# Attention and a two-product layer on one core: weights converted four tiles at a time, and the switch to three-product arithmetic made earlier

## The chip, the core and the metric

The program runs on one core of a Trainium2 chip. The core has a matrix engine (PE), a vector engine (DVE), a scalar engine (ACT), GpSimd (POOL) and a queue engine (SP) that issues the DMAs. Each engine works through its own list of instructions in order; semaphores hold an instruction until another engine or a DMA has done its part. The metric is the device time of one execution in microseconds, lower is better.

## The reference

```python
def _attn_ref(q, k, v):                # 8 batches, 8 heads, 576 positions, 64 wide
    scores = 1/sqrt(64) * q @ k.T      # heads 0-3: a causal window of 32
    scores = where(masks, scores, -1e9)  # heads 4-7: 128 wide, every 4th position
    attn = softmax(scores)
    return attn @ v

x = attention output as (4608, 512)
h = x @ w_in                           # (512, 2048)
g = where(h > 0, h, exp(min(h, 0)) - 1)
out = g @ w_out                        # (2048, 512)
```

The weights come to the chip as 64-bit floating-point numbers and are made into 32-bit numbers by integer operations on their two halves.

## The kernel before, in words

**Chunks and tiles.** The 4608 rows of x are worked through as nine chunks (c = 0 to 8) of 512. The 2048 hidden columns are sixteen tiles (f = 0 to 15) of 128. For each chunk and tile `gemm1` makes the 128x512 hidden block h in one PSUM bank (h0 or h1), `elu` makes g of it, and `gemm2` adds g's product with the rows f of w_out into four PSUM banks (o_ps), two tiles later (LAG = 2): the order on PE is gemm1 of tile f, then gemm2 of tile f - 2. After a chunk's sixteenth gemm2, `store` copies the four banks out on ACT (L420) into buffers `o`, and SP sends each to memory (L421). The attention of batch c + 1 is worked in between, as pieces behind chosen tiles of chunk c: the tuple `when` (L508) names the tiles behind which the scores of head pairs 0 and 1, their outputs, the scores of pairs 2 and 3, and their outputs stand. A scores piece has two halves on PE; between them stands a one-element copy on ACT, `nothing` (L326), which the second half waits for.

**Two kinds of product.** A product of 32-bit numbers is either one plain matrix product, or three of numbers split into a high part (rounded to fp32r) and the rest (low): high by high, high by low, low by high. `split_w` makes the two parts of a weight (a cast on ACT, L136, a subtraction on DVE, L137), `split_x` those of x (L363, L364), and the end of `elu` those of g (`gh` on ACT, L405, `gl` on DVE, L406). In chunk 0 the first products use plain ones below tile F1 = 9 and the second below F2 = 14; all others use three.

**Converting.** `load_w(k)` loads a "pair" k: two 128x512 blocks of weights, in the order in which they are needed (mostly the w_in of tile k + 1 and the w_out of tile k - 1). `magnitude(k)` takes the upper words' absolute value on ACT (L103, 128x1024), `convert(k)` has four DVE operations of 128x1024 (L111, L113, L114, L116). The raw words lie in eight buffers r0 to r7, four of which hold inputs of the first attention before; pair 8 is loaded over pair 0's once that is converted. In chunk 0 the loop converts up to AHEAD = 4 tiles ahead. What chunk 0 leaves unsplit is split in chunk 1.

**What sets the order.** The framework lays every engine's list out beforehand by a timeline of its own; `inorder` keeps an instruction in program order, and `tc.issue_after` puts one behind another. PE's products are all in program order. Tiles of a pool (`fp` for e, gh, gl, h, o) come from buffers in turn, and the first writer of a buffer waits for the last reader before.

## Time and profile before

| what | value |
|---|---|
| median of 3 runs | 904.67 us (904.6 to 905.83) |
| the profiled execution, its own time | 905.6 us |
| its span, first to last instruction | 903.7 us |
| PE busy | 883.6 us (98%) |
| DVE busy | 581.0 us (64%) |
| ACT busy | 376.7 us (42%) |
| mean granted PE clock | 0.996 |

The profiled execution took 0.93 us more than the median, and 1.9 us of it lie around the span. A PE busy share counts pipelined products by ends that are modelled, so PE's pace is read from the distance between starts.

### The profile page before, as it was taken

How to read it: one execution, taken by the hardware profiler on the slowest of the kernel's cores; microseconds unless marked ns; L12 is line 12 of the kernel's file. 1: busy time of each engine (PE TensorE's matmuls, PEld its weight loads, DVE VectorE, ACT ScalarE, POOL GpSimd, SP SyncE). 2: the span in 40 equal slices, each digit the busy share in tenths (PEclk: the TensorE clock that was granted, in tenths of full speed). 3: DMA queues.
4: the chain of work that ended last, by engine and by line, in shares of the span. 5: the costliest groups of instructions: out<-in, count | busy, mean ns of one | idle time of the engine just before them, and what ended most of it. 6: DMA issues, size and time to landing. Idle time of an engine off the chain costs nothing.

```text
span 903.7 us, 15468 instructions
## 1 busy us (share of the span) xinstructions
PE 883.6 (98%) x6540; PEld 695.3 (77%) x6540; DVE 581.0 (64%) x999; ACT 376.7 (42%) x750; POOL 6.0 (1%) x12
## 2 busy tenths in 40 slices
PE   6899999999999999999999999999999999999998
PEld 4544657788878887888788878888788888888886
DVE  5899999966485847694687559574859433343332
ACT  3755767434533343434443343434434432233222
POOL 2000000000000000000000000000000000000000
PEclk8999999999999999999999999999999999999999
DMA  9964103020122013111202111210210010001001
GB/s 341 406 228 145 45 19 100 19 90 1 43 94 89 2 36 102 36 55 36 102 7 84 36 48 54 90 34 2 102 37 1 1 47 1 1 0 47 1 1 46
DMA packets 23796, 59.35 MB, mean 66 GB/s; under 512 B 2640, under 2 KB 2736, under 8 KB 23728
## 3 DMA queue, kind: packets, MB, share of 16 engines
q1 hardware_dynamic: 23728, 58.37, 18.9%
q8 instruction: 51, 0.84, 0.4%
q14 instruction: 17, 0.14, 0.0%
HBM read 48.92 MB, written 9.44 MB: 65 GB/s over the span
## 4 chain that ended last, share of the span: by engine, by line
PE 82%; DVE 8%; DMA 5%; issue 2%; ACT 2%; SPq 0%; ACTq 0%; DVEq 0%
PE h L83 41%; PE o_ps L83 38%; PE a_ps L83 3%; DMA r<-w_out 2%; DVE a L116 1%; DVE a L114 1%; DMA out<-o 1%; DVE a L111 1%; DVE pt L304 1%; DMA r<-w_in 1%; DVE gh L397 1%; DVE r L137 1%; ACT o L420 1%; DVE a L113 1%; DMA kt<-k 1%
## 5 line engine op out<-in xcount | busy, mean ns | idle before, releaser
L83 PE MATMUL o_ps<-a,gh 128*128 128x512 f32 x816 | 267.8, 418 | 0.0
L83 PE MATMUL h<-xh,r 128*128 128x512 f32 x792 | 266.2, 394 | 0.5 <-DVE gh L397 0.5
L83 PEld LDWEIGHTS o_ps<-a,gh 128*128 128x128 f32 x816 | 152.8, 188 | 50.4 <-issue 22.0
L401 DVE TENSOR_SCALAR e<-e 128x512 f32<-128x512 f32 x128 | 54.6, 426 | 191.8 <-ACT e L392 189.9
L83 PEld LDWEIGHTS h<-xh,r 128*128 128x128 f32 x792 | 148.6, 188 | 35.6 <-DVE gh L397 2.1
L83 PE MATMUL h<-xl,r 128*128 128x512 f32 x412 | 160.6, 390 | 0.0
L405 ACT CAST gh<-e 128x512 fp32r<-128x512 f32 x130 | 80.9, 622 | 177.0 <-DVE e L402 176.7
L83 PE MATMUL o_ps<-a,gl 128*128 128x512 f32 x352 | 136.9, 389 | 0.0
L406 DVE TENSOR_TENSOR gl<-e,gh 128x512 fp32r<-128x512 f32 x130 | 89.6, 689 | 71.9 <-ACT gh L405 41.5
L392 ACT ACTIVATE e<-h 128x512 f32<-128x512 f32 x144 | 89.4, 621 | 103.6 <-PE h L83 100.9
L390 ACT COPY h<-h 128x512 f32<-128x512 f32 x96 | 56.2, 585 | 117.7 <-PE h L83 117.6
L304 DVE STREAM_TRANSPOSE pt<-sm 32x384 f32<-32x384 f32 x168 | 95.4, 568 | 2.2
L83 PE MATMUL o_ps<-r,gh 128*128 128x512 f32 x304 | 96.2, 389 | 0.0
L402 DVE SCALAR_TENSOR_TENSOR e<-h,e 128x512 f32<-128x512 f32 x128 | 88.2, 689 | 3.5
L83 PEld LDWEIGHTS h<-xl,r 128*128 128x128 f32 x412 | 77.3, 188 | 17.0 <-issue 1.2
L83 PE MATMUL h<-xh,a 128*128 128x512 f32 x256 | 85.5, 395 | 0.0
L83 PEld LDWEIGHTS o_ps<-a,gl 128*128 128x128 f32 x352 | 66.1, 188 | 13.8
L83 PEld LDWEIGHTS o_ps<-r,gh 128*128 128x128 f32 x304 | 57.1, 188 | 11.8
L83 PE MATMUL o_ps<-r,gl 128*128 128x512 f32 x168 | 65.5, 390 | 0.3 <-DVE gl L406 0.3
L83 PEld LDWEIGHTS h<-xh,a 128*128 128x128 f32 x256 | 48.0, 188 | 11.0
L83 PE MATMUL h<-xl,a 128*128 128x512 f32 x128 | 50.0, 391 | 0.0
L289 ACT ACTIVATE sm<-sm 96x768 f32<-96x768 f32 x24 | 20.4, 849 | 45.0 <-DVE sm L288 45.0
(100 smaller groups left out, 751.4 us busy)
## 6 DMA issues: line engine op xcount, KB each, us to landing
vt<-v SPq DMA_DIRECT2D x30, 384.0 KB, 3.6
kt<-k SPq DMA_DIRECT2D x30, 304.0 KB, 4.6
qt<-q SPq DMA_DIRECT2D x30, 288.0 KB, 3.8
r<-w_in SPq DMA_DIRECT2D x16, 512.0 KB, 8.0
r<-w_out SPq DMA_DIRECT2D x16, 512.0 KB, 8.2
out<-o SPq DMA_DIRECT2D x32, 256.0 KB, 2.8
out<-xl SPq DMA_DIRECT2D x4, 256.0 KB, 2.1
r<-v SPq DMA_DIRECT2D x2, 384.0 KB, 8.3
```

The lines of the kernel that those rows point to most:

```text
L83: return inorder(nc.tensor.matmul(*args, **kw))
L111: keep(nc.vector.tensor_scalar(out=a, in0=a, scalar1=TINY, scalar2=None, op0=ALU.max))
L113: keep(nc.vector.tensor_scalar(out=au, in0=au, scalar1=0x07FFFFFF, scalar2=3, op0=ALU.bitwise_and, op1=ALU.logical_shift_left))
L114: keep(nc.vector.scalar_tensor_tensor(out=au, in0=hi, scalar=0xC0000000, in1=au, op0=ALU.bitwise_and, op1=ALU.bitwise_or))
L289: nc.scalar.activation(out=sm, in_=sm, func=AF.Exp, scale=0.125)
L304: last_transpose[b] = nc.vector.transpose(out=tr[ks, :, cs], in_=sm[cs, :, rs]).ins
L390: nc.scalar.copy(out=h, in_=h_ps)
L392: nc.scalar.activation(out=e, in_=h_ps, func=AF.Exp)
L401: nc.vector.tensor_scalar(out=e, in0=e, scalar1=1.0, scalar2=-1.0, op0=ALU.min, op1=ALU.add)
L402: nc.vector.scalar_tensor_tensor(out=e, in0=h_ps, scalar=0.0, in1=e, op0=ALU.max, op1=ALU.add)
L405: nc.scalar.copy(out=gh, in_=e)
L406: nc.vector.tensor_tensor(out=gl, in0=e, in1=gh.bitcast(F32), op=ALU.subtract)
```

## The change

Three groups of edits.

*Conversion by two pairs.* The raw words now lie in four buffers of two pairs each (NR = 4), and so do the converted weights (a0 to a7). `convert(j)` works on pairs 2j and 2j + 1 in one set of four operations of 128x2048. Pairs 0 and 1 are still converted in pieces before tile 0's products, pairs 2 and 3 in two pieces of 128x1024 behind the hidden block of tile 0. `magnitude` stays at one operation for each pair. AHEAD goes from 4 to 3 and the loop advances by two tiles. Both pairs of a buffer are loaded once the buffer's whole set of earlier readers is done.

*Three products earlier.* F1 goes from 9 to 7 and F2 from 14 to 11. Weights of two more first products and three more second products are split in chunk 0, and tiles 11 to 13 of chunk 0 get their `gl`. Chunk 1's splits wait in addition for a hidden block of late in chunk 0.

*Later chunks.* For chunks 2 to 6 the attention pieces stand behind tiles 2, 7, 8 and 13 (before 1, 6, 7 and 12). The buffers for `e` are four and serve the output copies as well, where there were three for each.

```diff
@@ -34,8 +34,8 @@
 NC = DM // P
-AHEAD = 4
-NR = NF // 2
-NE = 4
+AHEAD = 3
+NR = NF // 4
+NE = 2
 LAG = 2
-F1 = 9
-F2 = 14
+F1 = 7
+F2 = 11
 NEG = -1.0e9
@@ -52,3 +52,3 @@
     xp = ctx.enter_context(tc.tile_pool(name="xp", bufs=1))
-    fp = ctx.enter_context(tc.tile_pool(name="fp", bufs=3))
+    fp = ctx.enter_context(tc.tile_pool(name="fp", bufs=4))
     ps_first = ExitStack()
@@ -67,3 +67,4 @@
-    early = [wst.tile([P, 4 * DM], F32, name=f"r{NR - NE + i}") for i in range(NE)]
+    early2 = [wst.tile([P, 2, 4 * DM], F32, name=f"r{NR - NE + i}") for i in range(NE)]
+    early = [early2[i // 2][:, i % 2, :] for i in range(2 * NE)]
     for z in pt:
@@ -71,3 +72,3 @@
-    raw, full2, full = [None] * NF, [None] * NF, [None] * 2 * NF
+    raw2, raw, full4, full2, full = [None] * (NF // 2), [None] * NF, [None] * (NF // 2), [None] * NF, [None] * 2 * NF
@@ -86,3 +87,5 @@
-        raw[k] = wst.tile([P, 2, DM], I64, name=f"r{k % NR}")
+        if k % 2 == 0:
+            raw2[k // 2] = wst.tile([P, 4, DM], I64, name=f"r{k // 2 % NR}")
+        raw[k] = raw2[k // 2][:, k % 2 * 2:k % 2 * 2 + 2, :]
         if behind is not None:
@@ -93,5 +96,5 @@
-    def halves(k):
+    def words(j):
-        u = raw[k].rearrange("p t c -> p (t c)").bitcast(U32).rearrange("p (c two) -> p c two", two=2)
+        u = raw2[j].rearrange("p t c -> p (t c)").bitcast(U32).rearrange("p (c two) -> p c two", two=2)
         return u[:, :, 0], u[:, :, 1]
@@ -99,11 +102,14 @@
     def magnitude(k):
-        pair = full2[k] = wst.tile([P, 2, DM], F32, name=f"a{k}")
+        j, part = k // 2, slice(k % 2 * 2 * DM, (k % 2 + 1) * 2 * DM)
+        if k % 2 == 0:
+            full4[j] = wst.tile([P, 4, DM], F32, name=f"a{j}")
+        full2[k] = full4[j][:, k % 2 * 2:k % 2 * 2 + 2, :]
         for t in range(2):
-            full[need[2 * k + t]] = pair[:, t, :]
-        return nc.scalar.activation(out=pair.rearrange("p t c -> p (t c)"), in_=halves(k)[1].bitcast(F32), func=AF.Abs)
+            full[need[2 * k + t]] = full2[k][:, t, :]
+        return nc.scalar.activation(out=full4[j].rearrange("p t c -> p (t c)")[:, part], in_=words(j)[1][:, part].bitcast(F32), func=AF.Abs)
-    def convert(k, keep=lambda ins: ins, part=slice(0, 2 * DM)):
+    def convert(j, keep=lambda ins: ins, part=slice(0, 4 * DM)):
-        lo, hi = [u[:, part] for u in halves(k)]
-        a = full2[k].rearrange("p t c -> p (t c)")[:, part]
+        lo, hi = [u[:, part] for u in words(j)]
+        a = full4[j].rearrange("p t c -> p (t c)")[:, part]
         au = a.bitcast(U32)
@@ -118,3 +124,3 @@
-    spaces = [[f"r{i}", 4] for i in range(NR)] + [["a-1", 2]]
+    spaces = [["a-1", 4]] + [[f"r{i}", 8] for i in range(NR)]
     taken = {}
@@ -139,4 +145,4 @@
             wh[need[2 * k + t]], wl[need[2 * k + t]] = h[:, t - t0, :], l[:, t - t0, :]
-        if all(wh[need[2 * k + t]] is not None for t in range(2)):
-            spaces.append([f"a{k}", 2])
+        if all(wh[need[k // 2 * 4 + t]] is not None for t in range(4)):
+            spaces.append([f"a{k // 2}", 4])
@@ -386,3 +392,3 @@
     def elu(h_ps, c, f):
-        e = fp.tile([P, TC], F32, name="e", bufs=3)
+        e = fp.tile([P, TC], F32, name="e")
         if 0 < c < B - 1:
@@ -418,3 +424,3 @@
         for t in range(TC // P):
-            o = fp.tile([P, DM], F32, name="o", bufs=3) if c < NCH - 1 else xp.tile([P, DM], F32, name=f"xl{t}")
+            o = fp.tile([P, DM], F32, name="e") if c < NCH - 1 else xp.tile([P, DM], F32, name=f"xl{t}")
             nc.scalar.copy(out=o, in_=o_ps[t])
@@ -473,3 +479,3 @@
         elif what[0] in "BCD":
-            last_conversion = convert(i, inorder, {"B": slice(0, DM), "C": slice(DM, 2 * DM), "D": slice(0, 2 * DM)}[what[0]])
+            last_conversion = convert(i // 2, inorder, {"B": slice(0, DM), "C": slice(DM, 2 * DM), "D": slice(2 * DM, 4 * DM)}[what[0]])
         elif what[0] == "G":
@@ -484,3 +490,3 @@
     load_v(NPAIR)
-    for j in range(NR - NE, NR + 2):
+    for j in range(2 * (NR - NE), 2 * NR + 2):
         load_w(j)
@@ -507,12 +513,15 @@
-        when = () if c == 0 or c >= B - 1 else (0, 6, 7, 13) if c == 1 else (1, 6, 7, 12)
+        when = () if c == 0 or c >= B - 1 else (0, 6, 7, 13) if c == 1 else (2, 7, 8, 13)
         for f in range(NF):
             while c == 0 and ready < min(NF, f + AHEAD):
-                with tc.issue_after(below[-1] if below else last_copy.ins):
-                    magnitude(ready)
-                with tc.issue_after(last_conversion.ins):
-                    last_conversion = convert(ready)
-                if ready + NR < NF:
-                    load_w(ready + NR)
-                ready += 1
+                for j in (ready, ready + 1):
+                    with tc.issue_after(below[-1] if below else last_copy.ins):
+                        magnitude(j)
+                if f > 0:
+                    with tc.issue_after(last_conversion.ins):
+                        last_conversion = convert(ready // 2)
+                for j in (ready, ready + 1):
+                    if j + 2 * NR < NF:
+                        load_w(j + 2 * NR)
+                ready += 2
             if c == 0 and f == F1 - 3:
@@ -523,3 +532,3 @@
-                with tc.issue_after(last_transpose[1] if split < 2 else last_x):
+                with tc.issue_after(last_transpose[1] if split < 2 else last_x), tc.issue_after(hidden[-3]):
                     if left:
@@ -528,2 +537,7 @@
             pend.append((c, f, elu(gemm1(c, f), c, f)))
+            if (c, f) == (0, 0):
+                for part in slice(0, 2 * DM), slice(2 * DM, 4 * DM):
+                    with tc.issue_after(last_conversion.ins), tc.issue_after(hidden[-1]):
+                        last_conversion = convert(1, part=part)
             if c == 0 and F1 <= f + 2 <= NF:
```

On **ACT**, around the end of chunk 2 and the start of chunk 3 (`h` copies and `e` exponentials belong to hidden blocks, `o` or `e<-o_ps` are the output copies of the chunk just ended). Before:

```order
L392 ACTIVATE e<-h 128x512 [waits Activation_49]
L405 CAST gh<-e 128x512 [waits DVE_49]
L390 COPY h<-h_3229 128x512 [waits PE_49]
L392 ACTIVATE e<-h 128x512 [waits Activation_49]
L420 COPY o<-o_ps 128x512 [waits DMAHW0_49,PE_49]
L420 COPY o<-o_ps 128x512 [waits DMAHW1_49,PE_49]
L420 COPY o<-o_ps 128x512 [waits DMAHW2_49,PE_49]
L405 CAST gh<-e 128x512 [waits DVE_49]
L420 COPY o<-o_ps 128x512 [waits DMAHW7_49,PE_49,Activation_49]
L326 COPY nothing<-h_3278 96x1 [waits PE_49]
L289 ACTIVATE sm<-sm 96x768 [waits DVE_49]
```

With the change:

```order
L396 COPY h<-h_3222 128x512 [waits PE_49]
L398 ACTIVATE e<-h 128x512 [waits Activation_49]
L426 COPY e<-o_ps 128x512 [waits PE_49] x2
L426 COPY e<-o_ps 128x512 [waits DVE_49,PE_49]
L411 CAST gh<-e 128x512 [waits DVE_49]
L426 COPY e<-o_ps 128x512 [waits DMAHW7_49,PE_49,Activation_49]
L396 COPY h<-h_3269 128x512 [waits PE_49]
L398 ACTIVATE e<-h 128x512 [waits DVE_49,Activation_49]
L411 CAST gh<-e 128x512 [waits DVE_49]
L332 COPY nothing<-h_3310 96x1 [waits PE_49]
L295 ACTIVATE sm<-sm 96x768 [waits DVE_49]
```

`nothing` has moved behind the next tile's h copy, exponential and gh. The fourth output copy waits for a DMA in both: the buffer it takes is again that of the first output copy.

On **DVE**, in chunk 0 around the softmax of the third head pair of the second batch (a the converted weights, r_844, r_987 and r_1066 split weights, sm, nmx and sums the second attention, gh the hidden blocks). Before, with tile 9's hidden block as the seventh row:

```order
L397 SCALAR_TENSOR_TENSOR gh<-h_932,e 128x512
L206 TENSOR_SCALAR sums<-sums 96x12
L116 SCALAR_TENSOR_TENSOR a_926<-r_530,a_926 128x1024
L111 TENSOR_SCALAR a_963<-a_963 128x1024
L137 TENSOR_TENSOR r_987<-a_848,r_987 128x512
L207 RECIPROCAL sums<-sums 96x12
L397 SCALAR_TENSOR_TENSOR gh<-h_969,e 128x512
L113 TENSOR_SCALAR a_963<-a_963 128x1024
L208 TENSOR_TENSOR sm<-sm,sums 96x768
L137 TENSOR_TENSOR r_987<-a_926,r_987 128x512
L114 SCALAR_TENSOR_TENSOR a_963<-r_546,a_963 128x1024
L304 STREAM_TRANSPOSE pt_80<-sm 32x12x32 x6
```

With the change (the same hidden block, tile 9's, is the last row; ahead of it stand six transposes):

```order
L119 TENSOR_SCALAR a_906<-a_906 128x2048
L287 TENSOR_REDUCE nmx<-sm 96x12
L403 SCALAR_TENSOR_TENSOR gh<-h_913,e 128x512
L120 SCALAR_TENSOR_TENSOR a_906<-r_510,a_906 128x2048
L290 TENSOR_SCALAR nmx<-nmx 96x12
L122 SCALAR_TENSOR_TENSOR a_906<-r_510,a_906 128x2048
L212 TENSOR_SCALAR sums<-sums 96x12
L213 RECIPROCAL sums<-sums 96x12
L214 TENSOR_TENSOR sm<-sm,sums 96x768
L143 TENSOR_TENSOR r_844<-a_906,r_844 128x512
L310 STREAM_TRANSPOSE pt_80<-sm 32x12x32 x6
L403 SCALAR_TENSOR_TENSOR gh<-h_952,e 128x512
```

The operations on pairs 10 and 11 are joined (a_906, 128x2048), the maximum's scaling (nmx, the row that ACT's exponentials of that head pair wait for) stands behind the first long operation of the conversion, and tile 9's hidden block behind the softmax and the transposes of that head pair, which it stood ahead of before.

## The prediction

> **What bounds the kernel now.** I began with the busy shares, then the stages, then who waited for whom, then the chain of work that ended last.
>
> ```profile
> PE 883.6 (98%) x6540; PEld 695.3 (77%) x6540; DVE 581.0 (64%) x999; ACT 376.7 (42%) x750; POOL 6.0 (1%) x12
> ```
>
> PE is the bound over the whole span. The stages (start and end, length, then busy time of PE, weight loads, DVE, ACT and POOL with instruction counts, granted clock, DMA share, GB/s) say two different things:
>
> ```profile
> 60.00:80.00 20.00, 20.00 (x68) 8.92 (x66) 19.83 (x30) 11.56 (x37) 0.00 (x0) 1.00 0.51 178
> 80.00:100.00 20.00, 20.00 (x146) 11.11 (x146) 19.83 (x29) 13.05 (x39) 0.00 (x0) 1.00 0.17 51
> 300.00:400.00 100.00, 99.07 (x785) 81.71 (x784) 67.67 (x121) 42.16 (x78) 0.00 (x0) 1.00 0.16 52
> ```
>
> In chunk 0 PE and DVE are both full: 20.00 and 19.83 of 20 us. So a gain on PE there is worth only what DVE lets through. In a later chunk DVE has a third of its time free, and PE misses 0.93 us in 100 us, one hole per chunk. The clock is 1.00 in each. The waits name that hole (total, times, longest):
>
> ```profile
> PEld h L83 <- ACT nothing L326: 5.4, 5, 1.1
> ...
> ACT o L420 <- DMA out<-o: 5.2, 7, 0.9
> ```
>
> Five times PE waits for the one-element copy `nothing`; the output copies wait for their own store. The chain of waits shows how they hang together (start, length), in chunk 3:
>
> ```profile
> 339.38 2.73 PE h L83 x12
> ...
> 343.29 0.58 ACT o L420
> ...
> 343.89 2.21 DMA out<-o
> ...
> 346.20 0.59 ACT o L420
> 346.79 0.06 ACT nothing L326
> ...
> 347.59 2.97 PE h L83 x13
> 350.56 2.72 PE o_ps L83 x12
> ...
> 380.11 2.72 PE o_ps L83 x12
> ...
> 387.42 2.72 PE o_ps L83 x12
> ```
>
> Hidden tile 1 starts at 339.38. The last second product of chunk 2 and the first half of the scores follow. On ACT stand first the output copies; the fourth needs the buffer of the first, whose store is on its way for 2.21 us, and `nothing` is queued behind it. PE's second half of the scores starts only then. From 339.38 to the second product at 350.56 are 11.18 us; three tile products take 3 x 2.72 = 8.16, so this scores piece cost 3.02 us. The same piece behind tile 7 lies between 380.11 and 387.42 with two products: 7.31 - 5.44 = 1.87. The hole is 3.02 - 1.87 = 1.15 us, and 5 x 1.15 = 5.75 us, which agrees with the 5.4 us of the wait.
>
> **Later attention: -5.75 us.** Behind tile 2 the scores stand one gemm1 and one gemm2 later, and `nothing` stands on ACT behind the next h copy, exponential and gh. The fourth output copy still waits for a store, since it takes the first one's buffer again; so that wait remains, but is covered. With the chain's times: the copy ends at 346.79; PE would now run tile 2's first product from 344.8 to 347.5 and the next second product from there, which needs the fourth bank in its last quarter, at 347.5 + 2.04 = 349.5. That is 2.7 us after the copy. Queued behind the copy is only tile 2's h copy, needed before the next first product at 350.2; it is done by 348.1. If this cover failed, up to 1.15 us for each of five chunks would come back. The distances between scores and outputs stay five tiles, the loads move with them, and x for the next chunk is copied out by tile 13 with two tiles (10.9 us) to go, so I cost these moves at nothing. Sharing four buffers between e and the output copies lets tile 3's e wait for the second store, which has landed four us earlier.
>
> **Chunk 0, PE's side.** Plain and three-product tiles start at (start, length, count):
>
> ```profile
> 84.54 3.60 PE L83 MATMUL h<-x,a 128*128 128x512 f32 x8
> 87.97 3.60 PE L83 MATMUL o_ps<-a,gh 128*128 128x512 f32 x8
> ...
> 98.51 0.79 PE L83 MATMUL h<-xh,r 128*128 128x512 f32 x1
> ...
> 104.71 0.79 PE L83 MATMUL h<-xh,r 128*128 128x512 f32 x1
> ```
>
> A plain product of a tile takes 87.97 - 84.54 = 3.43 us, a mixed pair (first product of three, second plain) 104.71 - 98.51 = 6.20, and a pair of three-product ones 2 x 2.72 = 5.44. Tiles 7 and 8 go from 6.86 to 6.20, tiles 11 to 13 from 6.20 to 5.44: 1.3 + 2.3 = 3.6 us of PE. At the start there is something more:
>
> ```profile
> 39.70 3.70 PE L83 MATMUL h<-x,a 128*128 128x512 f32 x8 [0.96 <-DVE gh L397]
> ```
>
> Tile 2 waited 0.96 us for tile 0's hidden block, ahead of which stood a 0.6 us operation on the next pair; that now stands behind it, so PE starts some 0.6 us sooner.
>
> **Chunk 0, DVE's side.** Conversion by group, then single ones and DVE's waits (start, length; in brackets the idle time before):
>
> ```profile
> L114 DVE SCALAR_TENSOR_TENSOR a<-r,a 128x1024 uint32<-128x1024 uint32 x15 | 18.3, 1220 | 0.2
> ...
> L111 DVE TENSOR_SCALAR a<-a 128x1024 f32<-128x1024 f32 x15 | 10.3, 686 | 0.8 <-ACT a L103 0.8
> ```
>
> ```profile
> 25.88 0.42 DVE L111 TENSOR_SCALAR a<-a 128x512 f32<-128x512 f32 x1
> ...
> 26.79 0.69 DVE L114 SCALAR_TENSOR_TENSOR a<-r,a 128x512 uint32<-128x512 uint32 x1
> ...
> 49.28 0.69 DVE L111 TENSOR_SCALAR a<-a 128x1024 f32<-128x1024 f32 x1
> ...
> 50.75 1.21 DVE L114 SCALAR_TENSOR_TENSOR a<-r,a 128x1024 uint32<-128x1024 uint32 x1
> 51.87 0.95 DVE L208 TENSOR_TENSOR sm<-sm,sums 96x768 f32<-96x768 f32 x1
> ...
> 124.05 0.69 DVE L397 SCALAR_TENSOR_TENSOR gh<-h,e 128x512 f32<-128x512 f32 x1 [0.67 <-ACT e L394]
> ...
> 135.80 0.69 DVE L406 TENSOR_TENSOR gl<-e,gh 128x512 fp32r<-128x512 f32 x1 [1.04 <-ACT gh L405]
> ...
> 139.38 0.69 DVE L399 SCALAR_TENSOR_TENSOR e<-h,e 128x512 f32<-128x512 f32 x1 [0.75 <-ACT e L394]
> 139.99 0.62 DVE L364 TENSOR_TENSOR xl<-x,xh 128x448 fp32r<-128x448 f32 x1
> ```
>
> No row has a 128x2048 one. From 512 to 1024 columns the two-operand kind goes from 0.69 to 1.22 us and the one-operand kind from 0.42 to 0.69; carried on, 2048 takes 2.28 and 1.23. The queue gains less than durations say: the operation at 50.75 lasts 1.21 and the next starts 1.12 later, so 0.09 of each is overlapped. Two sets of four cost 2 x (2 x 1.13 + 2 x 0.60) = 6.92, one joined set 2 x 2.19 + 2 x 1.14 = 6.66. Six of the eight sets are joined (pairs 0 to 3 stay in pieces): 6 x 0.26 = 1.6 us saved. The bounds for a 2048 operation are this slope below and twice the 1024 row above (2.44 and 1.38), which is 12 x 0.16 + 12 x 0.15 = 3.7 us more; I take the slope, as two sizes lie on it.
>
> [...] By durations the fixed part is 0.69 - 0.53 = 0.16 us, and 24 fewer operations would save 3.8 us; the distance of 1.12 to the next start says that part of it is hidden already. [...]
>
> Added are splits and `gl`:
>
> ```profile
> L406 DVE TENSOR_TENSOR gl<-e,gh 128x512 fp32r<-128x512 f32 x130 | 89.6, 689 | 71.9 <-ACT gh L405 41.5 <-PE o_ps L83 29.6 <-PE h L83 0.7
> ...
> L269 ACT ACTIVATE sm<-sm,nmx 96x64 f32<-96x64 f32 x48 | 16.0, 339 | 8.1 <-DVE nmx L284 8.0
> ...
> L137 DVE TENSOR_TENSOR r<-a,r 128x1024 fp32r<-128x1024 f32 x4 | 4.8, 1221 | 0.0
> ...
> L137 DVE TENSOR_TENSOR r<-a,r 128x512 fp32r<-128x512 f32 x7 | 4.8, 682 | 0.0
> ```
>
> By the end of chunk 0's last tile DVE has three more splits of 1024 columns and one fewer of 512 (3 x 1.13 - 0.6 = 2.8 us), and three more `gl` (3 x 0.6 = 1.8). ACT's share of this, the casts, falls into its free time (13.05 of 20 us busy between 80 and 100). Net, DVE gets 2.8 + 1.8 - 1.6 = 3.0 us more. Its own waits change too: 0.67, 1.04 and 0.75 above go or shrink, but `nmx` of the third head pair now comes behind a 2.2 us operation, and the twelve exponentials that wait for it, at 0.33 apiece 4 us, outlast the other 2.2 us one by 1.8.
>
> Walking the new DVE order from 49.28, where both orders have done the same work, with these distances, the hidden block of tile 9 comes at 105.5, when PE has been ready for tile 11 since 103.5; tile 13's `gl` comes 1.4 us after PE wants it; and the last part of x for chunk 1 comes at about 142 where it was at 139.99 + 0.62 = 140.6. PE, ready for chunk 1's first product at 139.4, is held in its eighth of twelve matmuls and ends at 142 + 5 x 0.23 = 143.2. Before, the next product started here:
>
> ```profile
> 143.67 2.72 PE o_ps L83 x12
> ```
>
> So the PE gain of 3.6 + 0.6 us comes out as 0.5 us. The weights' later loads I cost at nothing: pairs 4 and 5 can be loaded only once the first attention has left their joint buffer, where pair 5 alone went before,
>
> ```profile
> 29.46 0.33 SPq L92 DMA_DIRECT2D r<-w_in  x1
> ```
>
> and are wanted by DVE at 49.3, twenty us later. From both sides: -4.7 us if DVE kept up (3.6 + 0.6 and half a us that PE waited late in the chunk),
>
> ```profile
> 133.08 0.50 PE L83 MATMUL h<-xh,r 128*128 128x512 f32 x1 [0.50 <-DVE gh L397]
> ```
>
> and +3.2 with the dear 2048 operations.
>
> **Chunk 1: -0.4 us.** Three of its splits are done already. Tile 4's two products took
>
> ```profile
> 164.83 2.73 PE h L83 x12
> ...
> 170.86 2.72 PE h L83 x12
> ```
>
> 6.03 us instead of 5.44, while `gl` was late behind splits: 0.59 us lost. I take 0.4, since DVE starts chunk 1 no earlier than before; the bounds are 0 and 0.6.
>
> **Sum.** -5.75 - 0.5 - 0.4 = -6.65: the profiled execution's 905.6 becomes 898.95. It was 0.93 above the median of the runs, so the median should go from 904.67 to 898.0.
>
> **Rivals.**
>
> *PE alone sets chunk 0.* For it: 3.6 us of matmul work are gone for certain, and two of DVE's idle spells lay in waits for ACT that fall away. Against: DVE is at 19.83 of 20 and gets work. Then chunk 0 gives 4.7, and the time is 893.8. Chance 0.13.
>
> *The hole only moves.* The fourth output copy still waits for a store, and if the shared buffers or the copies' place on ACT hold PE's second product of tile 0, the piece stays at 3 us in five chunks: 905.6 - 0.9 - 0.93 = 903.8. For it: the DMA wait stands in the new order too. Against: 2.7 us of room. Chance 0.10; with it goes 0.06 for half of it, about 901.
>
> *DVE falls behind in chunk 0: slower.* One mechanism: hidden blocks of tiles 3 to 13 stand behind 2.2 us operations where they stood behind 1.13, and as a hidden block frees the PSUM bank of the tile after next, each delay of 1.1 us would go on to PE, 11 x 1.1 = 12 us. Against: a hidden block now has some 10 us from its product to its deadline, and it decides only once that room is used up; two tiles of the walk (9 and 13) are at that point. From a loss of 6.2 us in chunks 0 and 1 it outweighs the hole; at 12 us the time is 904.67 - 5.75 + 12 = 910.9. Chance 0.05.
>
> *The change doesn't do what it says* in part already: the joined conversion leaves pairs 0 to 3 in pieces, and the buffers still alias. Both are in the sum.
>
> **How the numbers follow.** The forecast has 0.66, the others 0.13, 0.16 together, and 0.05. The range goes from 893.5 (PE alone) to 902.5 (dear conversions, or most of the hole kept) and leaves out most of the hole's rival, the slower one and a little below: about 0.15 to 0.2. A change is told from none here from about 0.2%, 1.8 us. Faster: the forecast, PE alone and the halved hole, with most of the unmoved hole left to same: 0.89. Same 0.06, slower 0.05.
>
> **What would show it.** In the profile after: no wait of PE for `nothing` in chunks 2 to 6, and 1.9 us for their scores behind tile 2, while ACT still waits for stores about 0.9 us per chunk; PE idle 0.0 to 0.3 us per later chunk. Conversions of 128x2048 at 2.28 and 1.23. In chunk 0 DVE full and PE waiting for DVE 2 us before tile 11 and 1 to 2 us around tiles 13 to 15. Chunk 1's first second product (143.67 above) half a us sooner. It is wrong if a later chunk still takes as long as before, if chunk 0 ends several us sooner (DVE was not the limit), or later than 145.

## The result and the profile after

The changed kernel takes 899.84 us (median of five runs, 897.85 to 901.5) beside 905.05 for the kernel before: ratio 0.994, 95% interval 0.9925 to 0.996, so 0.6% faster. The forecast was 898.0, with a range from 893.5 to 902.5. The profiled execution took 899.32 us with a span of 897.5. Busy time over the span, and then the stages of before again (columns as there):

```profile
PE 880.3 (98%) x6560; PEld 700.1 (78%) x6560; DVE 580.5 (65%) x977; ACT 378.3 (42%) x752; POOL 6.0 (1%) x12
```

```profile
60.00:80.00 20.00, 17.40 (x60) 8.41 (x59) 19.90 (x23) 10.43 (x34) 0.00 (x0) 0.91 0.60 224
80.00:100.00 20.00, 20.00 (x155) 12.35 (x154) 16.59 (x22) 9.47 (x33) 0.00 (x0) 1.00 0.16 51
300.00:400.00 100.00, 100.00 (x790) 82.60 (x789) 68.80 (x127) 41.14 (x77) 0.00 (x0) 1.00 0.16 52
```

A later chunk is now full: 100.00 of 100 us where it was 99.07. Chunk 0 is not: between 60 and 80 PE misses 2.6 us that it did not miss before, and the granted clock is 0.91.

**The hole is gone.** The chain of waits in chunk 3, and ACT's timeline at the same place (start, length; in brackets the idle time before):

```profile
345.98 2.72 PE o_ps L84 x12
...
350.30 2.98 PE h L84 x13
353.28 2.72 PE o_ps L84 x12
```

```profile
345.67 0.59 ACT L426 COPY e<-o_ps 128x512 f32<-128x512 f32 x1 [1.88 <-DMA out<-e]
...
349.37 0.15 ACT L332 COPY nothing<-h 96x1 f32<-96x1 f32 x1
```

From second product to second product are 7.30 us, two tile products are 5.44, so the scores cost 1.86 (3.02 before). ACT still waits 1.88 us for a store, and PE does not see it: the copy ends at 346.26, and the bank is needed in the last quarter of the product that starts at 345.98, at 348.0. `nothing` is queued behind the same copy, with the next tile's h copy, exponential and gh between them; gh ends at 349.25 (348.63 + 0.62) and `nothing` starts at 349.37, without holding PE.

**A new hole in chunk 0.** PE's timeline, then DVE's, then the stages of 2 us:

```profile
38.26 3.70 PE L84 MATMUL h<-x,a 128*128 128x512 f32 x8 [0.35 <-DVE gh L403]
...
66.26 1.72 PE L84 MATMUL a_ps<-pt,vt 128*64 128x96 f32 x24 [2.60 <-issue]
67.91 4.84 PE L84 MATMUL o_ps<-a,gh 128*128 128x512 f32 x8
72.59 3.60 PE L84 MATMUL h<-x,a 128*128 128x512 f32 x8
...
95.74 1.21 PE L84 MATMUL a_ps<-pt,vt 128*64 128x96 f32 x24
96.88 3.70 PE L84 MATMUL o_ps<-a,gh 128*128 128x512 f32 x8
```

```profile
54.62 1.27 DVE L370 TENSOR_TENSOR xl<-x,xh 128x512 fp32r<-128x512 f32 x2
55.82 2.29 DVE L122 SCALAR_TENSOR_TENSOR a<-r,a 128x2048 uint32<-128x2048 uint32 x1
...
59.16 1.29 DVE L370 TENSOR_TENSOR xl<-x,xh 128x512 fp32r<-128x512 f32 x2
60.37 3.47 DVE L310 STREAM_TRANSPOSE pt<-sm 32x384 f32<-32x384 f32 x6
63.87 1.23 DVE L119 TENSOR_SCALAR a<-a 128x2048 uint32<-128x2048 uint32 x1
65.01 0.68 DVE L403 SCALAR_TENSOR_TENSOR gh<-h,e 128x512 f32<-128x512 f32 x1
65.61 1.01 DVE L285 TENSOR_TENSOR sm<-a_ps,masks_sb 96x384 f32<-96x384 f32 x2
```

```profile
64.00:66.00 2.00, 0.00 (x0) 0.00 (x0) 2.00 (x3) 1.97 (x4) 0.00 (x0) 1.00 0.52 213
66.00:68.00 2.00, 1.74 (x25) 1.55 (x25) 2.00 (x3) 1.43 (x2) 0.00 (x0) 0.71 0.03 8
68.00:70.00 2.00, 2.00 (x3) 0.97 (x4) 2.00 (x3) 0.40 (x1) 0.00 (x0) 0.50 0.45 121
70.00:72.00 2.00, 2.00 (x5) 0.88 (x5) 2.00 (x2) 0.00 (x0) 0.00 (x0) 0.94 0.19 75
```

The profile puts PE's idle 2.60 us down to "issue", as if nothing held it. The attention products write the two banks a_ps that hold the second head pair's scores, and those are free only when DVE's mask adds (L285) have read them: the first of the two runs from 65.61 to 66.15, and PE starts at 66.26. The transposes that make the products' other input (pt) had ended at 63.84. Ahead of the mask adds now stand the four xl of chunk 0's x (2.4 us), since the first product of three comes two tiles sooner, and operations on 2048 columns. Behind the wait the granted clock falls to 0.50; by these stages it is halved for (1 - 0.71) x 4 + 2 + (1 - 0.94) x 4 = 3.4 us; the two groups at 66.26 and 67.91 take 1.72 and 4.84 us where such groups take 1.21 and 3.70, 1.65 us lost.

What follows stands on ACT, DVE and PE, in this order:

```profile
82.39 0.60 ACT L398 ACTIVATE e<-h 128x512 f32<-128x512 f32 x1 [3.37 <-PE h L84]
82.88 1.13 ACT L142 CAST r<-a 128x512 fp32r<-128x512 f32 x2
```

```profile
83.52 0.69 DVE L143 TENSOR_TENSOR r<-a,r 128x512 fp32r<-128x512 f32 x1 [1.42 <-ACT r L142]
...
100.08 0.17 DVE L212 TENSOR_SCALAR sums<-sums 96x12 f32<-96x12 f32 x1 [1.97 <-ACT sm L275]
...
137.31 0.69 DVE L412 TENSOR_TENSOR gl<-e,gh 128x512 fp32r<-128x512 f32 x1
```

```profile
138.05 0.50 PE L84 MATMUL o_ps<-r,gl 128*128 128x512 f32 x1 [0.99 <-DVE gl L412]
...
142.64 0.50 PE L84 MATMUL h<-xl,r 128*128 128x512 f32 x1 [0.38 <-DVE xl L370]
143.91 0.62 PE L84 MATMUL o_ps<-r,gh 128*128 128x512 f32 x2
```

ACT waits 3.37 us for the late product, the casts of the next split are queued behind that exponential, and DVE, which has hardly any time to spare here, stands still for 1.42 us. The later wait of 1.97 us, for the exponentials of the softmax (`sums`), is not due to the late tile: a run below in which the tile is not late has it too (1.98). At the end of chunk 0 PE waits for DVE again, 0.99 us for a `gl` and 0.38 us for the last part of x.

### The profile page after: what moved, and what is told of

It is laid out like the page before. It is cut to its first block, busy times and chain, and to the rows that moved or that the text cites. A ratio compares the mean times of both kernels' runs of the same rounds, so it can differ in the third digit from the quotient of the medians.

```text
span 897.5 us, 15525 instructions
## 1 busy us (share of the span) xinstructions
PE 880.3 (98%) x6560; PEld 700.1 (78%) x6560; DVE 580.5 (65%) x977; ACT 378.3 (42%) x752; POOL 6.0 (1%) x12
## 4 chain that ended last, share of the span: by engine, by line
PE 89%; DVE 7%; ACT 2%; issue 1%; DMA 0%; POOL 0%; SPq 0%; DVEq 0%; ACTq 0%
PE h L84 43%; PE o_ps L84 41%; PE a_ps L84 4%; DVE r L143 1%; DVE pt L310 1%; DVE a L120 1%; DVE a L122 1%; ACT pt L269 1%; DVE a L117 0%; ACT sm L275 0%; PE a L84 0%; DMA kt<-k 0%; PE b L84 0%; DVE a L119 0%; DVE xl L370 0%
## 5 line engine op out<-in xcount | busy, mean ns | idle before, releaser
L84 PE MATMUL o_ps<-a,gh 128*128 128x512 f32 x728 | 238.2, 416 | 0.0
L84 PE MATMUL h<-xh,r 128*128 128x512 f32 x696 | 231.9, 394 | 0.0
L84 PEld LDWEIGHTS o_ps<-a,gh 128*128 128x128 f32 x728 | 136.9, 189 | 43.6 <-issue 18.1
L84 PEld LDWEIGHTS h<-xh,r 128*128 128x128 f32 x696 | 130.6, 188 | 29.4 <-issue 1.0
L84 PE MATMUL h<-xl,r 128*128 128x512 f32 x348 | 135.7, 390 | 0.4 <-DVE xl L370 0.4
L84 PE MATMUL o_ps<-r,gh 128*128 128x512 f32 x424 | 130.8, 390 | 0.0
L84 PE MATMUL o_ps<-a,gl 128*128 128x512 f32 x320 | 124.5, 389 | 0.0
L84 PEld LDWEIGHTS o_ps<-r,gh 128*128 128x128 f32 x424 | 79.3, 188 | 16.7 <-ACT e L426 0.2
L84 PE MATMUL o_ps<-r,gl 128*128 128x512 f32 x212 | 82.6, 390 | 1.0 <-DVE gl L412 1.0
L84 PE MATMUL h<-xh,a-1_778 128*128 128x512 f32 x144 | 48.9, 400 | 0.0
```

Source lines behind the costliest of these rows:

```text
L84: return inorder(nc.tensor.matmul(*args, **kw))
```

## The experiments

All ran five timed rounds (one run 11, one 10) beside the kernel before, whose median was 905.1 to 905.4 in each group. For chunks 0 and 1 the table reads three starts from PE's timeline: tile 0's first product (h), the second product of tile 14 of chunk 0 (A) and that of tile 4 of chunk 1 (B). For the changed kernel h is 28.52, A the row at 143.91 above, and B 178.50. The difference A - h is chunk 0 without the start, which wanders between kernels with the same instructions there (h lies between 28.27 and 29.10 where the conversions are joined, and between 28.93 and 29.66 where they are not); from B to the end of the span no DVE work of chunk 0 is left.

| run | median us | ratio, 95% interval | A - h | B - A | B - h | B to end |
|---|---|---|---|---|---|---|
| before | 905.05 | | 114.15 | 35.35 | 149.50 | 724.8 |
| changed | 899.84 | 0.9925 to 0.9960 | 115.39 | 34.59 | 149.98 | 719.0 |
| attention back | 905.65 | 0.9997 to 1.0015 | 115.42 | 34.61 | 150.03 | 725.9 |
| attention alone | 899.26 | 0.9924 to 0.9949 | 114.13 | 35.40 | 149.53 | 719.1 |
| split of x two tiles later | 899.74 | 0.9922 to 0.9947 | 114.16 | 34.62 | 148.78 | 720.2 |
| no maximum | 898.25 | 0.9912 to 0.9937 | 112.83 | 36.19 | 149.02 | 719.1 |
| maximum twice | 909.17 | 1.0026 to 1.0055 | 121.83 | 38.44 | 160.27 | 719.9 |
| products from 9 and 13 | 899.29 | 0.9918 to 0.9946 | 112.19 | 36.61 | 148.80 | 719.7 |
| earlier products alone | 914.44 | 1.0080 to 1.0110 | 120.29 | 34.62 | 154.91 | 730.4 |
| POOL multiplies | 903.12 | 0.9966 to 0.9984 | 115.68 | 37.13 | 152.81 | 719.4 |
| not joined | 898.99 | 0.9919 to 0.9944 | 114.52 | 34.52 | 149.04 | 719.1 |
| products from 8 and 13 | 898.76 | 0.9914 to 0.9941 | 112.89 | 36.32 | 149.21 | 719.3 |
| products from 7 and 13 | 900.15 | 0.9933 to 0.9958 | 113.23 | 35.72 | 148.95 | 720.7 |
| not joined, 8 and 13 | 900.94 | 0.9938 to 0.9966 | 113.07 | 37.14 | 150.21 | 719.9 |

### Where the gain is: the attention undone, and alone

```diff
 changed kernel, attention back:
-when = ... (2, 7, 8, 13)
+when = ... (1, 6, 7, 12)
 kernel before, attention alone:
-when = ... (1, 6, 7, 12)
+when = ... (2, 7, 8, 13)
```

> The changed kernel with the attention of chunks 2 to 6 back behind tiles 1, 6, 7 and 12; e and the output copies go on sharing four buffers. My theory: the hole of 1.15 us is due to the place of the scores alone, so five of them come back: 899.84 + 5.75 = 905.6 us, and PE waits for the one-element copy five times again, some 5 to 6 us in all. Rival: the fourth shared buffer has helped as well, since tile 1's exponential and the copies now rotate through four; then the hole stays shorter, some 0.5 us a chunk, and the time is 902 to 903.

> The kernel before with only the attention of chunks 2 to 6 a tile later; conversions, first and second products and buffers as before (three for e, three for the output copies). My theory: 5 x 1.15 = 5.75 us less than the kernel before, 905.05 - 5.75 = 899.3 us; that is the whole gain of the changed kernel, and the other two parts together are worth nothing. Rival: the separate buffers, three for four output copies, leave part of the hole, and the time is above 901; or the parts in chunk 0 are worth something, and then the changed kernel is faster than this one by more than 0.5 us.

Undone: 905.65, 5.8 us more than the changed kernel, and the hole is back, in the waits of the whole run (total, times, longest):

```profile
PE h L84 <- ACT nothing L332: 5.6, 5, 1.9
```

Alone: 899.26, 5.9 us less than before and no slower than the changed kernel. The first theory holds in both, and the shared buffers neither help nor are needed for it. So the other two parts of the change, in chunks 0 and 1, are together worth nothing: their median is 0.6 us above that of the attention alone, inside the intervals.

### Where chunk 0's gain went: the split of x two tiles later

```diff
-if c == 0 and f == F1 - 3:
+if c == 0 and f == F1 - 1:
     split_x(0)
```

> The changed kernel with the split of x for chunk 0 (four operations of 128x512 on DVE, 0.6 us each) begun behind tile 6 instead of tile 4, so that it no longer stands ahead of the second attention's transposes and mask adds. Both theories: the mask adds at 65.61 come 2.4 us sooner, the attention products behind them begin at about 63.9 instead of 66.26, PE's idle 2.60 us shrink to under 0.3, and the granted clock stays at 1.00 where it fell to 0.50. Theory 1 (DVE sets the end of chunk 0): PE's 2.6 us and the 1.6 us of the slow clock come back as waits for DVE later in the chunk, except for the 1.4 us in which DVE itself waited for the late tile: 898.4 us (898 to 899.5). Theory 2 (this stall sets the end of chunk 0): all of 4.2 us is gained, 895.6 us.

The time did not move: 899.74, a little above theory 1's range. Nearly all of the steps came as theory 1 has them. The first mask add runs from 63.63 to 64.17, and the products start 0.10 us later, as they started 0.11 us behind it before; the clock is 1.00 there, and the next first product starts at 68.97 where it was 72.59. So the mask adds held PE. Then PE waits for DVE after all, at the place where the forecast's walk had it:

```profile
64.27 1.23 PE L84 MATMUL a_ps<-pt,vt 128*64 128x96 f32 x24 [0.16 <-PE h L84]
...
105.32 0.50 PE L84 MATMUL h<-xh,r 128*128 128x512 f32 x1 [2.15 <-DVE gh L403]
...
105.95 0.63 PE L84 MATMUL h<-xh,r 128*128 128x512 f32 x1
```

2.15 us for tile 9's hidden block, and behind it the clock is half again (0.50 for 3.4 us; 0.63 a matmul where it was 0.39): the stall is the same 2 us, 40 us later. Of 4.2 us 1.2 remain in A - h, which is what DVE's own waits fell by (1.42 us gone, 0.2 new). From B to the end it lost 1.1 us, 0.8 of them to a store that took longer in chunk 2, with `nothing` queued behind it; ACT there, and PE's wait (total, times, longest):

```profile
250.73 0.59 ACT L426 COPY e<-o_ps 128x512 f32<-128x512 f32 x1 [3.15 <-DMA out<-e]
```

```profile
PE h L84 <- ACT nothing L332: 0.8, 1, 0.8
```

The bank itself was free in time; it was `nothing`, behind the late copy, that came late. The same stands in three more of the runs below: where a store was waited for 2.9 to 3.0 us (maximum twice, 7 and 13, not joined with 8 and 13), PE waited 0.6 us for `nothing`. With 2.5 us (POOL multiplies) the profile names no such wait. So in these runs the cover held up to a store wait of about 2.4 us (an estimate: 3.15 - 0.8, 3.0 - 0.6).

### Less and more DVE work: the maximum left out, and done twice

```diff
 no maximum:
-keep(nc.vector.tensor_scalar(out=a, in0=a, scalar1=TINY, ..., op0=ALU.max))
 maximum twice:
+keep(nc.vector.tensor_scalar(out=a, in0=a, scalar1=TINY, ..., op0=ALU.max))
```

> The changed kernel without the first operation of each conversion, the maximum with the least normal number (it leaves out that part of the conversion, which bears on weights of zero or nearly zero only). It takes 6 x 1.13 us from DVE in the joined sets and some 2.5 us in the pieces, about 9 us of DVE in chunk 0. Theory 1 (DVE sets the end of chunk 0): every wait of PE for DVE in chunk 0 goes, 0.35 + 2.6 + 1.0 + 0.4 us and the 1.6 us of slow clock behind the second, 6 us: 894 us (893 to 895.5). Theory 2 (PE or ACT sets it): under 1.5 us, 898.5 or above.

> The changed kernel with the first operation of each conversion, the maximum, done twice (the result is the same): some 6 x 1.13 + 2.5 = 9.3 us more on DVE, the counterpart of the run without it, where 9 us less gave 1.6. Theory 1 (DVE alone sets the end of chunk 0): 9.3 us less the 3.4 us in which DVE waits for ACT, so 905.5 to 908. Theory 2 (DVE and PE about equally full, each with slack at other places): 901 to 904.

The second maximum made the kernel 9.3 us slower, more than theory 1 said, with 10.2 us more of DVE's busy time in the trace (590.7 against 580.5). Leaving the maximum out took 8.4 us from DVE (572.1) and made the kernel only 1.6 faster, where theory 1 said 6. As it was put, DVE alone setting the end, the theory falls. Without the maximum DVE has gaps, and other waits take their place; DVE, then PE:

```profile
93.47 0.69 DVE L401 SCALAR_TENSOR_TENSOR gh<-h,e 128x512 f32<-128x512 f32 x1 [3.50 <-ACT e L398]
```

```profile
128.11 0.51 PE L84 MATMUL o_ps<-r,gl 128*128 128x512 f32 x1 [1.75 <-DVE gl L410]
```

DVE stands 3.5 us for an exponential (ACT), and PE 1.75 us for a gl behind six transposes and then loses more to the half clock (0.50 for 3.4 us), in a chunk in which DVE was idle 11.0 of the 122 us from 28 to 150 (5.5 in the changed kernel). What is left there is not DVE's throughput but the order of its queue and ACT's. So in these two runs more work on DVE cost about its length and less work brought little. That the loss is as long as the added work is in part chance. It starts as early as tile 5, whose weights were converted 2.0 us before PE wanted them; PE's waits there (total, times, longest):

```profile
PE h L84 <- DVE a L123: 8.5, 2, 7.6
```

Up to there DVE has some 4 us of added work (an estimate from the lengths of the operations), but the last operation on these weights ends 11.2 us later (69.35 against 58.11): the list was laid out anew, with six transposes, two more xl, the mask adds and a hidden block ahead of it. The granted clock is 0.50 for 6.8 us at the wait of 7.6 us here, and for 3.4 us behind one of 1.98 us in chunk 1.

### Later products, joined conversions kept

```diff
-F1 = 7    F2 = 11
+F1 = 9    F2 = 13    (also 8 and 13, 7 and 13; there the split of x behind tile 6)
```

> The changed kernel with three-product first products from tile 9 (as before) and second products from tile 13 (14 does not fit the joined sets' memory); joined conversions and later attention stay. Against the changed kernel PE has 2 x 0.66 + 2 x 0.76 = 2.8 us more matmul work in chunk 0, and DVE two splits of 1024 columns and two gl less, 3.5 us. Theory 1 (DVE alone sets the end of chunk 0): the first product of chunk 1 starts 2 to 3 us sooner than in the changed kernel, of which the splits left for chunk 1 take back about one: 898.3 us (897.5 to 899). Theory 2 (PE and DVE are both full there, so that what the one gains the other loses): no sooner, 899.8 to 901.5.

> The changed kernel with three-product first products from tile 8 and second ones from tile 13, the split of x for chunk 0 behind tile 6. Against the run with 9 and 13, PE has 0.66 us less matmul work in chunk 0, and DVE does one split of 512 columns in chunk 0 instead of chunk 1. Theory 1 (DVE has no gap from the first conversion to the last split in chunk 1, so PE's work up to there does not count): 899.3 us, the same within half a us. Theory 2 (PE's work counts there as well): 898.6.

> The changed kernel with second products of three from tile 13 instead of 11, and the split of x for chunk 0 behind tile 6 instead of 4; first products of three from tile 7 as in the change. Against the run with 9 and 13, PE has 1.3 us less in chunk 0. Theory 1: 899.3 us, as with 9 and 13. Theory 2: 898.0. Against the changed kernel DVE has two splits of 1024 columns and two gl less in chunk 0, 3.5 us: the first product of chunk 1 should start 2 to 3 us sooner there by theory 1, and PE lose part of this again behind the splits left for chunk 1.

With 9 and 13 PE has 2.8 us more to multiply in chunk 0 and yet ends it 3.2 us sooner (112.19 against 115.39): there theory 1 is right. But the split of x stands behind tile 6 in these runs, and that alone brought 1.2 us above (114.16); to the 3.5 us of DVE work belong at most the other 2.0. Of the 3.2 us 2.0 go again in chunk 1 (36.61 against 34.59), where the splits are left over, and 0.7 later; the median is 0.55 us lower, within the scatter. 8 and 13 is 1.1 us below the changed kernel and the lowest median of a kernel with all of its work, but the intervals overlap; 7 and 13 is no better than the changed kernel, with 2.1 us of wait for tile 9's hidden block and a B to end 1.6 us longer. The times do not decide between the theories: 899.29 lies between them, 898.76 is nearer the second, and 900.15 is above both. No version is shown to beat the change. B - h is 148.8 to 149.2 in all three, and with the split of x later, without the maximum, and with the conversions not joined.

### What the joined conversions are worth

```diff
 kernel before, earlier products alone:
-F1 = 9    F2 = 14
+F1 = 7    F2 = 11
 and not joined, with the rest of the change:
-spaces = [[f"r{i}", 4] for i in range(NR)] + [["a-1", 2]]
+spaces = [["a-1", 4]] + [[f"r{i}", 4] for i in range(NR)]
-fp = ... bufs=3     e = ... name="e", bufs=3     o = ... name="o", bufs=3
+fp = ... bufs=4     e = ... name="e"             o = ... name="e"
-when = ... (1, 6, 7, 12)
+when = ... (2, 7, 8, 13)
```

> The kernel before with three-product first products from tile 7 and second ones from tile 11, and nothing else: conversions pair by pair, attention of later chunks where it was. PE has 3.6 us less, DVE 2.8 + 1.8 = 4.6 us more. Theory 1 (DVE alone sets the end of chunk 0): 1 to 3 us later than the kernel before, since DVE had about 2.5 us of waits there that can absorb work: 907 us. Theory 2 (both full): between no change and 2 us sooner, 903 to 905.

> All of the change but the joined conversions: the kernel before with the later attention, three-product first products from tile 7 and second ones from tile 11, four buffers shared by e and the output copies, and the memory that this frees given to the first splits (a space of four half-rows, taken first), as the changed kernel has it. Without that space, in the run of the earlier products alone, the first split had to wait 7 us for the raw weights of pair 8 to be converted; here it needn't. Theory 1 (DVE sets the end of chunk 0, and the joined conversions are worth the 1.6 us of DVE that they save there): 901.4 us (900.8 to 902.2), PE's wait of 7 us gone. Theory 2 (the longer operations cost as much in waits as they save): 899 to 900.3.

Alone, the earlier products cost 9 us, which neither theory had. In the profiled execution (915.95) B comes 5.4 us later and the time behind B is 5.6 us longer. ACT and PE show the first part:

```profile
82.78 1.14 ACT L136 CAST r<-a 128x512 fp32r<-128x512 f32 x2 [7.54 <-DVE a L116]
```

```profile
83.45 0.79 PE L83 MATMUL h<-xh,r 128*128 128x512 f32 x1 [7.14 <-ACT r L136]
```

The split of tile 7's weights is written into the raw weights' buffer r0, which pair 8 holds until DVE has converted it at 82.75. The changed kernel takes the space a-1 first, and has four half-rows there, with the memory that the shared buffers free; a part of the change that the prediction does not speak of. The second part lies in the old hole, which this kernel still has, with one long store in chunk 3 (ACT waits 2.7 us, PE 2.8) and the clock halved for (1 - 0.83) x 2 x 20 = 6.8 us in the same 20 us:

```profile
340.00:360.00 20.00, 17.20 (x200) 13.82 (x199) 9.12 (x16) 7.13 (x13) 0.00 (x0) 0.83 0.34 114
```

Why this kernel meets it is not shown; all five of its executions lie 7 to 10.6 us above the median of before, so something of it seems to come each time.

With the larger space and without joined conversions the time is 898.99: the wait of 7 us is gone, and the joined conversions are worth nothing (theory 2). They do save DVE the work that the forecast had: it is busy 580.5 us with them and 582.0 without, 1.5 us against 1.6. But its waits in chunk 0 are longer, 4.2 us (1.97, 1.42 and 0.8) against 0.8 here. That these waits are what eats the saving is argued from the sizes; no run shows it by itself.

Over the 24 operations that joining leaves out, 1.5 us is 1.5 / 24 = 0.06 us apiece. The forecast's estimate by durations, 3.8 us, took 0.16 us apiece: 0.69 us for 512 columns less the 0.53 that the next 512 add (1.22).

### Two attempts at less DVE work

```diff
 changed kernel:
-normalise(nc.vector, sm, sums, ...)
+normalise(nc.gpsimd if b == 1 else nc.vector, sm, sums, ...)
 not joined:
-F1 = 7    F2 = 11
+F1 = 8    F2 = 13
```

> The changed kernel with the multiplication of the probabilities of batch 1 by the reciprocal sums (128 rows replaced by 96, 768 columns, 0.95 us on DVE, four times in chunk 0) on POOL, which does the same for the first attention in 1.47 us. Theory 1 (DVE alone sets the end of chunk 0): 4 x 0.87 = 3.5 us off DVE come out for the most part, 896.5 to 898. Theory 2 (both full, and the order of the operations on DVE decides): under 1 us, 899 to 900.

> The run without joined conversions (later attention, shared buffers, the larger space for the first splits), with three-product first products from tile 8 and second ones from tile 13. In that run, with 7 and 11, PE waited 2.2 us for a gl at 134 and lost 1.7 us more to the half clock behind it. Here DVE has two splits of 1024 columns and two gl less in chunk 0, 3.5 us, and PE 0.66 + 1.5 = 2.2 us more. Theory 1 (DVE sets the end of chunk 0): the first second product of chunk 1 starts 1 to 2.5 us sooner than at 143.56 there, with no wait over 1 us and no half clock behind tile 2 on; part is lost in chunk 1; 898.3 us (897.7 to 899). Theory 2 (PE's added work counts): 899.5 to 901.

On POOL the multiplications made the kernel 3.3 us slower (903.12), above both theories. DVE did not get the 3.5 us: it is busy 581.3 us where it was 580.5. Beside each multiplication on POOL an operation on DVE took longer; DVE, then POOL, two of the four places:

```profile
52.12 3.33 DVE L120 SCALAR_TENSOR_TENSOR a<-r,a 128x2048 uint32<-128x2048 uint32 x1
...
97.92 1.84 DVE L143 TENSOR_TENSOR r<-a,r 128x512 fp32r<-128x512 f32 x1 [0.35 <-ACT r L142]
```

```profile
51.82 1.47 POOL L214 TENSOR_TENSOR sm<-sm,sums 96x768 f32<-96x768 f32 x1 [30.95 <-ACT a L109]
...
97.75 1.47 POOL L214 TENSOR_TENSOR sm<-sm,sums 96x768 f32<-96x768 f32 x1 [17.16 <-DVE sums L213]
```

Elsewhere the first takes 2.28 us and the second 0.68. The other two places are 2.96 for 2.29 and 2.18 for 1.22: in all 3.8 us longer, as much as was taken off. So this run does not test what less DVE work would bring. The written order of DVE's queue changed as well (six transposes now stand ahead of the last operation on tile 5's weights), and PE's longest waits in chunks 0 and 1 were these (total, times, longest):

```profile
PE h L84 <- DVE e L405: 2.7, 1, 2.7
PE h L84 <- DVE a L122: 1.7, 1, 1.7
```

In the last run chunk 0 ended 1.5 us sooner (113.07 against 114.52), with no wait over 1.0 us and the granted clock at 1.00, as theory 1 says, and chunk 1 lost 2.6. There stands the old hole, one chunk earlier; ACT:

```profile
157.77 0.59 ACT L420 COPY e<-o_ps 128x512 f32<-128x512 f32 x1 [2.37 <-DMA out<-e]
158.25 0.62 ACT L405 CAST gh<-e 128x512 fp32r<-128x512 f32 x1
```

The fourth copy of chunk 0's output waits for a store, the cast of the hidden block is queued behind it, and PE waits 1.13 us for that bank and 0.31 us later for a copy of h; the rest of the 2.6 us is lost in small pieces. The time, 900.94, lies in the range of theory 2 (899.5 to 901), but not for its reason, since chunk 0 did end sooner.

## Why the prediction was right, and where it was wrong

- **Later attention, -5.75 us: right**, in place and size. -5.8 undone, -5.9 alone; 719.0 against 724.8 from B to the end. The store wait stayed and was covered, as said. The room was misjudged: the prediction held the copy against the bank's deadline only (2.7 us, measured 1.7: 346.26 against 348.0) and had nothing but the h copy queued behind it. `nothing` is queued there too and comes late first, from a store wait of about 2.4 us on, half a us more than the 1.88 here; in four of the runs a store went beyond that.
- **PE's 3.6 us in chunk 0: right.** The time from h to B without PE's waits is 149.50 - 0.96 - 0.50 - 0.3 = 147.7 before and 149.98 - 0.35 - 2.60 - 0.99 - 0.38 - 1.65 = 144.0 after. All of the 3.7 us came back as waits, and 0.5 more. The 0.6 us at tile 2 came too (0.96 to 0.35).
- **2048 columns: right.** 2.29 and 1.22 us for 2.28 and 1.23.
- **"Walking the new DVE order ... the PE gain of 3.6 + 0.6 us comes out as 0.5 us": the step that failed.** A - h became 1.2 us longer, not 0.5 shorter. The walk asked of each hidden block and gl whether it comes in time, and not of the mask adds, which free the banks for the attention products. It also had no granted clock (0.50 for 3.4 us) and no wait of DVE for the late tile (1.42) in it. Its other points nearly held: `gh` of tile 9 at 105.52 (said 105.5), the wait for the exponentials 1.97 (1.8), tile 13's gl 0.99 late (1.4), the last xl ending at 142.6 (142). Counted from where both orders have done the same work, 49.28 before and 48.46 here, the first came 0.8 and the last 1.4 us later than said. The wait of 2 us ahead of tile 11 was not seen in the changed kernel, because PE was late itself, and stood there as soon as the split of x was moved (2.15).
- **Chunk 1, -0.4: right in place, too small.** B - A went from 35.35 to 34.59, -0.76, beyond the bound of 0.6. Tile 4's pair now takes 5.44 us, so all of its 0.59 us is gone; the other 0.17 lie elsewhere.
- **The correction of -0.93** from the profiled execution to the median was scatter taken for a constant: here the profiled execution is 0.52 below its median. Profile against profile the sum was nearly met, -6.3 us against -6.65, and that is partly luck: -5.84 from B on, +1.24 in chunk 0 and -0.76 in chunk 1 make -5.4, and most of the rest is a start 0.84 us sooner, which wanders by as much between runs.
- **The rivals.** The hole did not move. PE alone did not set chunk 0. DVE falling behind did not make the kernel slower, but the mechanism was there, at a bank the prediction had not named. What the two parts in chunks 0 and 1 do together was put at -0.9 us and is nothing that can be told from the scatter (+0.6).

## What to carry to other kernels

Where two engines are both full, count for each queue not only who feeds the bottleneck but who empties the buffers it writes next; a saving of 3.6 us on one went wholly into waits on the other. Making a full queue shorter was worth little here, since its order and the other engines' waits decided (8.4 us less work, 1.6 us gained), and making it longer cost about its length (10.2 us more work, 9.3 us slower). Work moved to another engine is saved only if the operations beside it keep their pace: here they took 3.8 us longer. A wait that cannot be removed can be put under two products of other work; the cover should be counted for everything queued behind the wait, and for the slowest store, not the usual one.

## What was unexpected of the hardware

A wait of PE cost more than its own length: in the changed kernel 1.65 us of half clock came on top of 2.60 us of idle time. From 28 us on the granted clock fell to 0.50 at ten waits in these runs; at the nine that stages of 1 us cover, it fell during the wait or at most 1.3 us behind its end. It was 0.50 for 3.4 us at waits of 1.75 us (no maximum), 1.98 (maximum twice), 2.15 (split of x two tiles later), 2.2 (not joined), 2.58 (attention back), 2.60 (changed) and 2.7 (POOL multiplies), and for 6.8 us at waits of 2.8 and 7.1 us (earlier products alone) and 7.6 us (maximum twice); of the 6.8 us, 3.5 at the wait of 7.1 and 3.9 at that of 7.6 lie in the wait itself. Half a clock for 3.4 us is up to 1.7 us of matmul work (1.65 in the changed kernel). It does not always come: waits of 0.99 (changed), 1.13 (not joined, 8 and 13) and 1.3 us (earlier products alone) had no such sequel, nor had one of 1.7 (POOL multiplies), one of 1.9 (attention back), nor this one in the run with 7 and 13 (the clock stays at 1.00), the same wait for the same hidden block as at 105.32 with the split of x later:

```profile
105.44 0.50 PE L84 MATMUL h<-xh,r 128*128 128x512 f32 x1 [2.13 <-DVE gh L403]
105.77 0.39 PE L84 MATMUL h<-xl,r 128*128 128x512 f32 x1
106.00 0.40 PE L84 MATMUL h<-xh,r 128*128 128x512 f32 x1
```

So nearly the same wait (2.15 and 2.13 us) went either way in two kernels that differ only in F2. What decides it, these runs do not show.

The 2.60 us of idle time that the profile of the changed kernel ends by "issue" were a wait for a PSUM bank read by DVE: when the read was moved 2 us earlier, they became 0.16, and in both cases PE started 0.1 us behind the end of that read.

A DVE operation beside a multiplication on POOL took 0.7 to 1.2 us longer in all four places (3.33 us for 2.28 at the first), so that moving work of 0.95 us each to POOL gave DVE nothing.
